# Router transposes in the score tiles' unused columns, the next unit's preparation dealt out anew, and another order for the first head

## The chip, the cores and the metric

The kernel runs on one core of a Trainium2 chip. The metric is the device time of one launch in microseconds; the runs before the change had a median of 1070.12 us (three runs, 1066.64 to 1074.0). TensorE is the matrix engine (PE; PEld its weight loads), VectorE is DVE, ScalarE is ACT, GpSimd is POOL, and SyncE (SP) issues most DMAs.

## The reference

Attention with a threshold feeds a mixture of experts, which feeds a dense layer. The shapes are 4 batches, 8 heads, 576 positions, 64 per head, all float32; 8 experts of 512 x 1024; and a last layer of 512 x 2048 and back.

```python
scores = scale * np.matmul(q, k.transpose(0, 1, 3, 2))
thresh = np.max(scores, axis=-1, keepdims=True) - tau
scores = np.where(scores >= thresh, scores, -1000000000.0)
scores = scores - np.max(scores, axis=-1, keepdims=True)
attn = np.exp(scores)
attn = attn / (np.sum(attn, axis=-1, keepdims=True) + 1e-09)
x = np.matmul(attn, v)                   # then (4*576) rows of 8*64
logits = x @ w_gate
expert_idx = np.argmax(logits, axis=1)   # one expert per row
# out[row] = gate_w[row] * (relu(x[row] @ w1[e]) @ w2[e])
h = x @ w_in
g = h - np.tanh(h)
return (g @ w_out).astype(np.float32)
```

## The kernel before

The program first runs attention (`Attn.run`), then the router's tables, then expert and last layer (`Mlp.run`). The experts need the router's result for all rows, so the second part starts when attention and the logits are done.

**Units and steps.** A unit is one head of two batches at once; there are 16 units. A unit has nine score tiles of 128 x 576, so attention has 144 steps, counted here as (unit, tile). A score tile lies in PSUM as two banks of 512 columns, of which the scores take 288 each; there are three such tiles. In the pass of the main loop with number `i`, these are emitted in this order: jobs of phase 0; `scores` of step i+2 on TensorE; jobs of phase 1; `smax` (maximum, VectorE) and `sexp` (exponential, ScalarE) of step i+1; every third pass `ev_m` (ScalarE copies transposed probabilities out of a score tile's columns 288 to 479); `smask` of step i (VectorE: threshold, multiplication and sum); `sthr`; jobs of phases 2 and 3. Each engine works through its own instructions in the order in which they are emitted, and the framework adds the waits. Two engines that read the same score tile in PSUM are put one behind the other.

**Jobs and their places.** `PL` gives each job of a unit a place (offset, phase), where the offset counts passes from the unit's step 0 (pass 9n for unit n). `PFIRST` replaces places for unit 0, `PLAST` for unit 15. The jobs:

- `lq`, `lk`, `lv`: loads of q, k and v for four heads at once, on SyncE's queue (4, 4 and 6 DMAs); the raw q and k tiles have three buffers.
- `dq` (GpSimd) writes q twice side by side; `hi1` (ScalarE) and `lo1` (GpSimd) split k into a high and a low part.
- `q0`, `m`, `q4`, `k0`, `k5`: transposes on TensorE, four of 128 x 128 (`m` two), into the single PSUM buffer `t`. `e...` is the evacuation on ScalarE, `f...` VectorE's low part of q. The buffer is free again after them.
- `vm`, `vn`, `vc`: maxima of v, their sum and a scale (VectorE, TensorE). `vw`, `vh` (ScalarE) scale v and copy it to fp16, `vl` (GpSimd) makes the low part.
- `se` (ScalarE) and `sl` (GpSimd) split the masked probabilities into two fp16 parts (`e16`, three buffers); `te` transposes them by DMA, three times a unit, also on SyncE's queue. `pv` (TensorE) multiplies by v; `po0` to `po2` (VectorE) put the normalised output into `X`; `st` stores it.
- `t0`, `v0`, `l0` and so on, once per pair of units, after the odd one: the router. `lg_tr` transposes three of nine blocks of `X` into the same buffer `t`, `lg_ev` copies them out (ScalarE, 384 columns), `lg_mm` multiplies by the gate's weights, `la` adds the logits up. They stand at offsets 23 to 32 of the odd unit n, so in units n+2 and n+3.

The places of `PL` that matter below, as step within the unit in which they run: `hi1` 3, `k0` and `ek0` 4, `k5` 4, `ek5` 5, `vw` 4, `vh` 5, `vl` 6, `q0` 7, `eq0` 8, `fq0` 8, `m` 8, `em` 0, `fm` 0, `q4` 0, `eq4` and `fq4` 1, `dq` 3, `lo1` 5.

At the start, `tau` is loaded by GpSimd's queue, unit 0's q by four DMAs of SyncE and its k by four of ScalarE; unit 0's transposes go into score tiles. At pass 4 `consts` makes the router's constants on GpSimd, and VectorE casts them.

## Time and profile before

| | |
|---|---|
| median of three runs | 1070.12 us (1066.64 to 1074.0) |
| the profiled execution | 1065.54 us, span 1063.8 us |
| busy share of the span: PE, DVE, ACT, POOL | 88%, 82%, 68%, 56% |
| mean granted clock of TensorE | 0.958 of full speed |

The profile is of one execution. Busy times are of the union of an engine's instructions. "Idle before" is the time that the engine stood ahead of an instruction, and the name behind the arrow is what ended that wait by the profile; where several things were waited for it is the one that the profile saw last, which need not be the one that mattered. Matmuls overlap, so a row of several matmuls is shorter than the sum of their durations.

### The profile page before, as it was taken

To read this page: it belongs to the slowest core of one execution; us is meant where nothing else is said; L and a number is where in the kernel's file an instruction comes from. 1 tells how busy PE (TensorE), PEld (TensorE's weight loads), DVE (VectorE), ACT (ScalarE), POOL (GpSimd) and SP (SyncE) were. 2 spreads that over 40 slices of the span, in tenths; PEclk is the share of its full clock that TensorE was granted. 3 is DMA by queue.
4 is the path that set the end of the run, shared out by engine and by line. 5 is a ranking of instruction groups with operands and counts; after the bars stand their busy time and mean duration, and the time that the engine had idled before them with its cause. 6 is when DMAs were issued, how large, how long until landed. Compare 5 with 4: busy or idle time off the path is not lost.

```text
span 1063.8 us, 20919 instructions
## 1 busy us (share of the span) xinstructions
PE 940.9 (88%) x7441; PEld 869.2 (82%) x7441; DVE 872.7 (82%) x1667; ACT 721.4 (68%) x1359; POOL 597.0 (56%) x581
## 2 busy tenths in 40 slices
PE   4577787887787498999999998999999999999997
PEld 4466676776786398999999997889999999999986
DVE  5789979888985678786777787999989889898893
ACT  4698998897995175666676766666666566556662
POOL 2788877887876211120011027786867768677763
PEclk9699988998998599999999999999999999999999
DMA  5599999998979497786898875120101001000000
GB/s 138 106 194 170 174 184 180 173 188 182 147 142 170 119 311 251 252 264 223 273 307 279 281 255 171 46 77 21 48 1 42 26 21 48 1 30 1 21 11 31
DMA packets 230826, 147.85 MB, mean 139 GB/s; under 512 B 161306, under 2 KB 207660, under 8 KB 230717
## 3 DMA queue, kind: packets, MB, share of 16 engines
q1 hardware_dynamic: 226957, 135.68, 51.2%
q0 software_dynamic: 3312, 10.49, 3.1%
q8 instruction: 60, 0.98, 0.4%
q14 instruction: 49, 0.40, 0.1%
q10 hardware_dynamic: 448, 0.30, 0.1%
HBM read 85.08 MB, written 23.60 MB: 102 GB/s over the span
## 4 chain that ended last, share of the span: by engine, by line
PE 46%; DVE 10%; DMA 5%; ACT 2%; issue 2%; another core or an unknown queue 0%; SPq 0%; POOL 0%; POOLq 0%; DVEq 0%; ACTq 0%
PE h L1054 22%; PE y L1137 15%; PE y L1109 8%; DMA raw<-in_moe_w_dram 3%; DVE w L1255 2%; DVE w L1256 2%; DMA wscr<-cm 1%; DVE w L1024 1%; DVE w L1253 1%; DVE tm L1254 1%; DVE w L1257 1%; PE t L1031 1%; ACT w L1022 0%; DVE cm L1185 0%; DVE keep L584 0%
## 5 line engine op out<-in xcount | busy, mean ns | idle before, releaser
L267 POOL TENSOR_TENSOR e<-em,e 128x1024 f16<-128x1024 f32 (+1 forms) x98 | 158.1, 1614 | 61.1 <-issue 29.9
L1252 POOL TENSOR_SCALAR tm<-u 128x384 uint8<-128x384 f32 x88 | 128.9, 1465 | 50.2 <-ACT u L1248 49.6
L1054 PE MATMUL h<-xa,w 128*128 128x256 f32 (+6 forms) x864 | 139.3, 311 | 3.3 <-DVE hbuf L1090 1.3
L1109 PE MATMUL y<-hbuf,w 128*128 128x256 f32 (+6 forms) x864 | 139.8, 310 | 0.3 <-ACT yo L1112 0.2
L1054 PEld LDWEIGHTS h<-xa,w 128*128 128x128 f32 x864 | 129.7, 193 | 5.2 <-DVE hbuf L1090 1.8
L255 DVE SCALAR_TENSOR_TENSOR em<-sps,n,e 128x576 f32<-128x576 f32 x144 | 116.8, 811 | 15.8 <-ACT et L287 4.8
L1109 PEld LDWEIGHTS y<-hbuf,w 128*128 128x128 f32 x864 | 127.4, 190 | 1.2 <-ACT yo L1112 0.8
L1248 ACT ACTIVATE u<-h 128x384 f32<-128x384 f32 x96 | 47.1, 491 | 117.5 <-PE h L1054 117.5
L242 ACT ACTIVATE e<-sps,n 128x576 f32<-128x576 f32 x144 | 108.5, 754 | 26.3 <-DVE n L236 26.1
L1255 DVE SCALAR_TENSOR_TENSOR w<-y,w 128x384 f32<-128x384 f32 x96 | 122.5, 1276 | 0.0
L1071 POOL DMA_INDIRECT xr<-rows,idx x26 | 27.3, 1049 | 163.8 <-PE t L1031 158.8
L236 DVE TENSOR_REDUCE n<-sps 128x1 f32<-128x576 f32 x144 | 107.2, 744 | 11.1 <-PE sps L228 11.1
L311 PE MATMUL ops<-vh,et 128*128 128x64 f16 (+1 forms) x2240 | 94.9, 200 | 20.7 <-DVE x L317 20.7
L1054 PE MATMUL h<-xk,w 128*128 128x384 f32 x576 | 109.2, 337 | 2.0 <-DVE w L1024 1.7
L311 PEld LDWEIGHTS <-et 128*128 128x128 f16 (+1 forms) x2240 | 84.1, 106 | 31.1 <-issue 25.7
L1054 PEld LDWEIGHTS h<-xk,w 128*128 128x128 f32 x576 | 102.1, 188 | 6.7 <-DVE w L1024 2.4
L1269 POOL TENSOR_TENSOR gl<-w,gh 128x384 fp32r<-128x384 f32 x83 | 84.6, 1019 | 38.8 <-ACT gh L1268 38.8
L228 PE MATMUL sps<-ka,qa 128*128 128x288 f32 x320 | 84.5, 356 | 19.2 <-DVE n L246 9.1
L263 ACT CAST e<-em 128x576 f16<-128x576 f32 x144 | 98.8, 687 | 3.3 <-DMA et<-e 1.2
L1024 DVE TENSOR_TENSOR w<-raw,w 128x1024 fp32r<-128x1024 f32 x68 | 84.0, 1238 | 20.6 <-ACT w L1022 19.9
L1022 ACT CAST w<-raw 128x1024 fp32r<-128x1024 f32 x72 | 75.4, 1050 | 18.7 <-DVE free L611 11.9
L1256 DVE SCALAR_TENSOR_TENSOR w<-y,w 128x384 f32<-128x384 f32 x96 | 77.7, 809 | 10.0
(237 smaller groups left out, 2207.6 us busy)
## 6 DMA issues: line engine op xcount, KB each, us to landing
raw<-in_moe_w_dram SPq DMA_DIRECT2D x64, 512.0 KB
cv<-in_moe_w_in_dram SPq DMA_DIRECT2D x16, 512.0 KB
cv<-in_moe_w_out_dram SPq DMA_DIRECT2D x16, 512.0 KB
wscr<-cm SPq DMA_DIRECT2D x32, 256.0 KB
raw<-wscr SPq DMA_DIRECT2D x16, 512.0 KB
xw<-yT SPq DMA_DIRECT2D x24, 192.0 KB
vv<-in_v_dram SPq DMA_DIRECT2D x8, 512.0 KB
raw<-in_k_dram SPq DMA_DIRECT2D x6, 512.0 KB
```

What stands on the lines that cost most here:

```text
L236: nc.vector.tensor_reduce(out=n[:, 0:1], in_=ps[:, :, 0:288], axis=AX.XY, op=ALU.max, negate=True)
L242: nc.scalar.activation(out=e, in_=ps[:, :, 0:288], func=AF.Exp, bias=n[:, 0:1])
L255: nc.vector.scalar_tensor_tensor(out=self.em[u, g][:, i].rearrange("p (a b) -> p a b", a=2), in0=ps[:, :, 0:288], scalar=n[:, 1:2], in1=e, ...
L263: self.nc.scalar.copy(self.e16[u, g][:, i, 0:S], self.em[u, g][:, i])
L267: eng.tensor_tensor(out=e16[:, r, S + 64:], in0=em[:, r, 0:512], in1=e16[:, r, 0:512], op=ALU.subtract)
L311: nc.tensor.matmul(o[q], lhsT=et[:, base + c, q], rhs=vh[:, a, j, c if c < 5 else c - 5, :], start=(n == 0), stop=(n == len(terms) - 1))
L1054: self.nc.tensor.matmul(out, lhsT=a, rhs=b, start=(i == 0), stop=(i == len(parts) - 1))
L1109: nc.tensor.matmul(self.ys[d], lhsT=a[:, f % 2, s], rhs=b, start=(f == 0 and i == 0), stop=(f == 7 and i == 2))
L1137: nc.tensor.matmul(self.ys[m], lhsT=a[:, s], rhs=b[:, f % 2], start=(f == 0 and i == 0), stop=(f == 15 and i == 2))
L1252: nc.gpsimd.tensor_scalar(out=mk, in0=u, scalar1=RCUT * RCUT, scalar2=None, op0=ALU.is_gt)
L1255: V.scalar_tensor_tensor(out=w, in0=y, scalar=b, in1=w, op0=ALU.add, op1=ALU.mult)
L1256: V.scalar_tensor_tensor(out=w, in0=z, scalar=d, in1=w, op0=ALU.add, op1=ALU.mult)
```

## The change

The router: for the pairs whose work ends before attention does (odd units 1 to 11), five passes (offsets 22, 23, 25, 26, 28) transpose two, two, two, two and one of the nine blocks of `X` into columns 288 to 415 of the two banks of the score tile that the pass fills, ahead of the scores; these passes are not those of the probability transposes. One pass later ScalarE copies them out, right behind that tile's exponential; another pass later the gate's matmuls run. The pairs of units 13 and 15 keep the old way.

The preparation of the next unit: new places in `PL`; loads of q and v are issued four and six passes earlier. As step within the unit in which they run: `dq` 1, `lo1` 4, `q0` 6, `eq0`, `fq0` 7, `m` and `hi1` 8, `em`, `fm` 0, `q4` 1, `eq4`, `fq4` 2, `vw` 3, `k0` 3, `ek0` and `k5` 4, `ek5` 5, `vh` 6, `vl` 7.

The first head: its q comes in two DMAs instead of four, the loads are emitted ahead of the activation table's load, q's doubling is cut between VectorE and GpSimd, k0 is transposed before `m` and `q4`, and `ek0` goes to ScalarE. The instructions that use tau stand behind the copies of zeros.

```diff
--- before.py
+++ after.py
@@ -27,6 +27,7 @@
...
 MLAG = 3, 4
+LGS = 22, 23, 25, 26, 28
...
@@ -47,22 +48,18 @@
...
+        self.load_qk(0, 0, 0, 1, nc.sync)
+        self.load_qk(0, 1, 0, 1, nc.scalar)
+        t = one.tile([128, 1], F32, name="tau")
+        nc.gpsimd.dma_start(out=t, in_=tau.to_broadcast([128, 1]))
...
         nc.vector.memset(w, 0.0)
         nc.scalar.activation(out=w, in_=w, func=AF.Exp)
-        t = one.tile([128, 1], F32, name="tau")
-        nc.gpsimd.dma_start(out=t, in_=tau.to_broadcast([128, 1]))
-        self.load_qk(0, 0, 0, 1, nc.sync)
-        self.load_qk(0, 1, 0, 1, nc.scalar)
...
-        self.g8 = one.tile([128, 1], F32, name="g8")
-        nc.vector.tensor_scalar(out=self.g8, in0=t, scalar1=0.0, scalar2=0.125, op0=ALU.is_ge, op1=ALU.mult)
-        self.ntau = one.tile([128, 1], F32, name="ntau")
-        nc.vector.tensor_scalar(out=self.ntau, in0=t, scalar1=0.0, scalar2=-1.0, op0=ALU.max, op1=ALU.mult)
...
@@ -71,6 +68,10 @@
                 tl = one.tile([128, 2 * QS], F32R, name=f"{nm}{i}")
                 nc.vector.tensor_copy(tl[:, S:S + 64], z)
                 lst.append(tl)
+        self.g8 = one.tile([128, 1], F32, name="g8")
+        nc.vector.tensor_scalar(out=self.g8, in0=t, scalar1=0.0, scalar2=0.125, op0=ALU.is_ge, op1=ALU.mult)
+        self.ntau = one.tile([128, 1], F32, name="ntau")
+        nc.vector.tensor_scalar(out=self.ntau, in0=t, scalar1=0.0, scalar2=-1.0, op0=ALU.max, op1=ALU.mult)
...
@@ -92,7 +93,7 @@
...
             if i == 0:
                 src = src.rearrange("h (p c) d -> p h c d", c=9)
-                for c in (slice(0, 5), slice(5, 9)):
+                for c in (slice(0, 5), slice(5, 9)) if e1 - e0 > 1 else (slice(0, 9),):
                     eng.dma_start(out=r[p, e0:e1, c], in_=src[:, :, c])
...
@@ -126,7 +127,12 @@
...
     def double(self, u):
         self.xq[u] = self.wk.tile([128, 9, 2, D], F32, tag="xq", name="xq")
-        (self.nc.gpsimd if u else self.nc.vector).tensor_copy(self.xq[u], self.raw[u, 0].unsqueeze(2).to_broadcast([128, 9, 2, D]))
+        src = self.raw[u, 0].unsqueeze(2).to_broadcast([128, 9, 2, D])
+        if u == 0:
+            self.nc.vector.tensor_copy(self.xq[u][:, 0:4], src[:, 0:4])
+            self.nc.gpsimd.tensor_copy(self.xq[u][:, 4:9], src[:, 4:9])
+        else:
+            self.nc.gpsimd.tensor_copy(self.xq[u], src)
...
@@ -198,8 +204,6 @@
...
         if what[0] in "qm":
             nc.scalar.copy(self.qview(self.QA[u % 2], what), self.pview(pf, what))
-        elif u == 0 and what == "k0":
-            nc.vector.tensor_scalar(out=ka[:, 0, 0:512], in0=flat, scalar1=self.g8, scalar2=None, op0=ALU.mult)
...
             nc.scalar.activation(out=ka[:, int(what == "k5"), 0:512], in_=flat, func=AF.Copy, scale=self.g8)
...
@@ -208,11 +212,13 @@
         self.nc.vector.tensor_tensor(out=self.qview(self.QB[u % 2], what), in0=self.pview(pf, what),
                                      in1=self.qview(self.QA[u % 2].bitcast(F32), what), op=ALU.subtract)
...
-    def scores(self, u, t, m=None):
+    def scores(self, u, t, m=None, l=None):
...
         ps = self.sp.tile([128, 2, 512], F32, tag="s", name="sps")
         if m:
...
+        if l:
+            l[0].lg_tr2(ps, *l[1:])
         qa, qb, ka = self.QA[u % 2], self.QB[u % 2], self.ka[u]
         if t == 4:
             terms = [(j, 512 + 64 * j) for j in range(2)]
@@ -331,17 +337,17 @@
...
-    PL = {"lq": (-21, 1), "lk": (-31, 2), "lv": (-12, 1), "dq": (-15, 1), "hi1": (-15, 3),
-          "lo1": (-13, 3), "q0": (-11, 1), "eq0": (-10, 1), "fq0": (-10, 2), "m": (-10, 2), "em": (-9, 1), "fm": (-9, 3), "q4": (-9, 3),
-          "eq4": (-8, 0), "fq4": (-8, 2), "k0": (-5, 0), "ek0": (-5, 0), "k5": (-5, 2), "ek5": (-4, 0),
-          "vm": (-7, 3), "vn": (-3, 1), "vc": (-3, 2), "vw": (4, 3), "vh": (5, 3), "vl": (6, 1),
+    PL = {"lq": (-25, 1), "lk": (-31, 2), "lv": (-18, 1), "dq": (-17, 1), "hi1": (-19, 1),
+          "lo1": (-14, 1), "q0": (-12, 1), "eq0": (-11, 0), "fq0": (-11, 2), "m": (-10, 1), "em": (-9, 0), "fm": (-9, 2), "q4": (-8, 1),
+          "eq4": (-7, 0), "fq4": (-7, 2), "k0": (-6, 1), "ek0": (-5, 0), "k5": (-5, 1), "ek5": (-4, 0),
+          "vm": (-7, 3), "vn": (-3, 1), "vc": (-3, 2), "vw": (3, 0), "vh": (6, 1), "vl": (7, 1),
           "se": (1, 2), "sl": (2, 0), "te": (4, 2), "pv": (11, 3), "po0": (14, 2),
           "po1": (20, 3), "po2": (20, 3), "de": (9, 3), "rc": (13, 1), "st": (32, 3), "t0": (23, 1), "v0": (24, 1), "l0": (31, 2),
           "t1": (24, 3), "v1": (24, 3), "l1": (28, 3), "t2": (29, 0), "v2": (29, 2), "l2": (30, 1), "la": (32, 2)}
...
-    PFIRST = {"dq": (-20, 2), "hi1": (-18, 0), "lo1": (-18, 1), "q0": (-17, 0), "eq0": (-16, 2), "fq0": (-16, 3),
-              "m": (-15, 3), "em": (-14, 1), "fm": (-14, 2), "q4": (-17, 3), "eq4": (-14, 0), "fq4": (-14, 2), "k0": (-15, 3), "ek0": (-13, 2),
-              "k5": (-14, 1), "ek5": (-12, 0),
+    PFIRST = {"dq": (-20, 2), "hi1": (-20, 3), "lo1": (-19, 0), "q0": (-18, 0), "k0": (-17, 1), "m": (-17, 2), "eq0": (-16, 0), "fq0": (-16, 1),
+              "ek0": (-16, 2), "em": (-15, 0), "q4": (-15, 1), "eq4": (-15, 2), "fm": (-15, 2), "k5": (-14, 1), "fq4": (-14, 2),
+              "ek5": (-14, 3),
               "lv": (-2, 1), "vm": (3, 3), "vn": (7, 1), "vc": (7, 2), "vw": (7, 3), "vh": (8, 3), "vl": (8, 3)}
...
@@ -355,7 +361,7 @@
     def run(self, units, moe=None):
...
-        sched = {}
+        sched, lgs = {}, {}
...
@@ -402,7 +408,13 @@
             at(b, "de", self.denom, u)
...
-            if moe and u % 2 == 1:
+            if moe and u % 2 == 1 and b + LGS[-1] + 2 < 9 * NU:
+                P, j = u // H, u % H // 2
+                for x, i in enumerate(LGS):
+                    lgs[b + i] = moe, P, j, x
+                    sched.setdefault((b + i + 2, 3), []).append((moe.lg_mm2, (P, j, x)))
+                at(b, "la", moe.lg_add, P, j)
+            elif moe and u % 2 == 1:
                 P, j = u // H, u % H // 2
...
@@ -419,12 +431,14 @@
...
             if 0 <= i + 2 < len(steps):
                 j = i - MLAG[0]
-                ps[i + 2] = self.scores(*steps[i + 2], (steps[j][0], steps[j][1] // 3) if j >= 0 and j % 3 == 0 else None)
+                ps[i + 2] = self.scores(*steps[i + 2], (steps[j][0], steps[j][1] // 3) if j >= 0 and j % 3 == 0 else None, lgs.get(i))
...
             if 0 <= i + 1 < len(steps):
                 nn[i + 1] = self.smax(ps[i + 1])
                 ee[i + 1] = self.sexp(ps[i + 1], nn[i + 1])
+            if i - 1 in lgs:
+                moe.lg_ev2(ps[i + 1], *lgs[i - 1][1:])
             j = i - MLAG[1]
             if 0 <= j < len(steps) and j % 3 == 0:
                 if i + 2 - MLAG[1] + MLAG[0] >= len(steps):
@@ -485,7 +499,7 @@
     def __init__(self, tc, at, wg, w1, w2, w_in, w_out, out, rows, yT, cp, dp):
...
-        self.cp, self.dp, self.xT, self.wgd = cp, dp, {}, wg
+        self.cp, self.dp, self.xT, self.xT2, self.wgd = cp, dp, {}, {}, wg
...
@@ -565,6 +579,20 @@
...
+
+    def lg_tr2(self, ps, P, j, x):
+        at = self.attn
+        for i in range(min(2, 9 - 2 * x)):
+            self.nc.tensor.transpose(ps[:, i, 288:416], at.X[4 * P + j][:, 2 * x + i], at.ident)
+
+    def lg_ev2(self, ps, P, j, x):
+        n = min(2, 9 - 2 * x)
+        self.xT2[x] = self.attn.wk.tile([128, 3, 128], F32, tag="xT", name="xT", bufs=3)
+        self.nc.scalar.copy(self.xT2[x][:, 0:n], ps[:, 0:n, 288:416])
+
+    def lg_mm2(self, P, j, x):
+        for i in range(min(2, 9 - 2 * x)):
+            self.nc.tensor.matmul(self.attn.lm[:, 2 * x + i], lhsT=self.xT2[x][:, i], rhs=self.wg[:, j], start=True, stop=True)
```

## Rows read from the trace of the kernel before

**Rows 1.** By unit: length, then PE, PEld, DVE, ACT, POOL busy, clock, DMA.
```profile
63.29:82.00 18.71, 13.45 (x213) 12.11 (x210) 16.41 (x44) 16.84 (x31) 15.85 (x17) 1.00 1.11 216
102.79:120.86 18.07, 15.29 (x235) 14.36 (x231) 16.66 (x45) 17.22 (x32) 15.27 (x16) 1.00 0.83 144
120.86:142.44 21.58, 16.45 (x219) 14.88 (x216) 16.38 (x45) 17.79 (x33) 16.47 (x18) 0.84 1.06 218
160.50:183.08 22.58, 16.56 (x221) 14.87 (x218) 20.00 (x51) 17.68 (x33) 16.11 (x18) 0.85 0.92 173
201.15:222.48 21.33, 16.98 (x224) 15.51 (x224) 16.53 (x44) 17.88 (x33) 16.48 (x18) 0.85 1.11 219
240.53:263.36 22.83, 17.06 (x221) 15.39 (x218) 19.75 (x52) 17.70 (x33) 16.26 (x18) 0.85 0.84 175
281.41:301.08 19.67, 15.34 (x220) 13.96 (x216) 16.39 (x45) 17.71 (x33) 16.50 (x18) 0.91 0.83 141
350.21:1063.80 713.59, 677.58 (x3905) 629.19 (x3905) 588.01 (x918) 440.00 (x854) 340.35 (x270) 0.98 0.39 126
```

**Rows 2.** Waits of VectorE in attention: total us, times, longest.
```profile
DVE n L236 <- PE sps L228: 9.6, 14, 1.5
DVE em L255 <- ACT et L287: 4.8, 11, 0.8
DVE pm L132 <- DMA vv<-in_v_dram: 4.8, 3, 2.4
```

**Rows 3.** The timeline of unit 5's middle: start, us, engine.
```profile
131.42 0.67 ACT L263 CAST e<-em 128x576 f16<-128x576 f32 x1 [0.99 <-POOL e L268]
...
133.45 0.90 PE L563 MATMUL lps<-ident,x 128*128 128x128 f32 x3 [2.40 <-ACT ka L204]
...
134.12 0.82 DVE L255 SCALAR_TENSOR_TENSOR em<-sps,n,e 128x576 f32<-128x576 f32 x1 [1.77 <-issue]
```

**Rows 4.** The timeline of unit 8's middle.
```profile
192.40 0.48 ACT L287 COPY et<-sps 128x384 f16<-128x384 f16 x1
...
192.91 0.82 DVE L255 SCALAR_TENSOR_TENSOR em<-sps,n,e 128x576 f32<-128x576 f32 x1 [0.36 <-ACT et L287]
...
193.33 0.85 ACT L146 ACTIVATE vv<-vv,sc 128x640 f32<-128x640 f32 x1
...
194.63 0.76 ACT L242 ACTIVATE e<-sps,n 128x576 f32<-128x576 f32 x1
...
195.48 0.82 DVE L255 SCALAR_TENSOR_TENSOR em<-sps,n,e 128x576 f32<-128x576 f32 x1 [0.55 <-POOL x L124]
...
195.82 0.76 ACT L150 CAST vh<-vv 128x640 f16<-128x640 f32 x1
```

**Rows 5.** Groups by line in attention: busy us, mean ns, idle before.
```profile
L255 DVE SCALAR_TENSOR_TENSOR em<-sps,n,e 128x576 f32<-128x576 f32 x140 | 113.6, 811 | 15.8 <-ACT et L287 4.8 <-POOL x L124 4.4 <-issue 4.1
...
L236 DVE TENSOR_REDUCE n<-sps 128x1 f32<-128x576 f32 x138 | 102.7, 744 | 9.6 <-PE sps L228 9.6
...
L228 PE MATMUL sps<-ka,qa 128*128 128x288 f32 x304 | 79.4, 353 | 16.0 <-DVE n L246 8.8 <-DVE em L255 6.6
...
L228 PE MATMUL sps<-ka,qb 128*128 128x288 f32 x304 | 66.5, 310 | 0.0
...
L563 PE MATMUL lps<-ident,x 128*128 128x128 f32 x63 | 14.6, 355 | 8.6 <-ACT ka L204 7.1 <-ACT xT L567 1.1 <-ACT et L287 0.4
...
L567 ACT COPY xT<-lps 128x384 f32<-128x384 f32 x21 | 10.2, 485 | 2.4 <-PE lps L563 2.3
```

**Rows 6.** The timeline as the constants begin.
```profile
27.93 1.13 POOL L129 COPY xq<-raw 128x1152 f32<-128x1152 f32 x1
...
29.66 0.17 DVE L503 CAST i<-i_i 128x8 f32<-128x8 int32 x1 [2.56 <-POOL i_i L502]
```

**Rows 7.** The timeline of the first loads.
```profile
7.59 2.57 SPq L96 DMA_DIRECT2D raw<-in_q_dram  x4
...
15.43 1.14 POOL L129 COPY xq<-raw 128x1152 f32<-128x1152 f32 x1 [12.83 <-DMA raw<-in_q_dram]
```

## The prediction, made before the change was run

> **What bounds the kernel now.** I read the stretch-by-stretch table first, cut where each attention unit's first mask starts. The part after attention takes 713.59 us and no line of it is edited [rows 1]; everything that can move lies ahead of it, and it starts when attention ends, so a microsecond saved there is one saved in all. In attention no engine is far from full. An even unit takes 18.07 us with ScalarE busy 17.22 and VectorE 16.66 (unit 4; units 6, 8, 10 and 12 repeat it within 0.02). An odd unit should differ little, yet units 5 and 9 take 21.58 and 21.33 with VectorE no busier (16.38 and 16.53), and TensorE's clock is 0.84 and 0.85 there instead of 1.00 [rows 1]. So an odd unit loses about 3.5 us that no engine works in.
>
> Next, who VectorE waits for: score tiles 9.6 us, the small copy of the transposed probabilities on ScalarE 4.8, the load of v 4.8 [rows 2]. The timeline of unit 5 then shows the chain: ScalarE's split waits 0.99 for its buffer, falls behind, and its evacuation of `k5` comes late; the router's transposes (L563) need the one preparation buffer in PSUM, wait 2.40 for that evacuation, and being ahead of the next scores in TensorE's queue they hold these up; VectorE's mask has already stood 1.77 [rows 3]. TensorE then restarts at the low level: three transposes take 0.90.
>
> Even units show the second cause [rows 4]. ScalarE gets v's scaling (0.85) and v's fp16 copy (0.76) in two neighbouring steps, with `ek0` and `ek5` between. Its exponentials come late and the masks wait 0.36 and 0.55. The 0.55 is put down to a GpSimd subtraction, but the exponential that this mask needs runs 194.63 to 195.39 and the mask starts at 195.48: ScalarE is the cause.
>
> **The change part by part.** *Router.* Of the eight odd units, six (1, 3, 5, 7, 9, 11) go the new way; their work falls in units 3 to 14. Nine transposes a pair stay nine, but move from the preparation buffer into columns 288 to 415 of score tiles, two at a time. What goes is the wait for that buffer: 8.6 us of TensorE idle ahead of L563 [rows 5], and with it the low clock. What comes: TensorE does two transposes between a tile's release and its scores. A transpose is 14.6/63 = 0.23 us of busy time, a tile's four score matmuls 2 x 79.4/304 + 2 x 66.5/304 = 0.96 [rows 5]; together 1.42. VectorE's own step (mask and maximum) is the room for it, 0.811 + 0.744 = 1.56 [rows 5], so it fits, barely, at the high clock. ScalarE copies five times (four of 256 columns, one of 128) instead of three times 384 columns at 485 ns [rows 5]. By columns alone nothing is added (9 x 128 either way); at 485 each it is 5 - 3 = 2 more, 0.97 a pair. I take 0.4 a pair, 0.2 a unit, nearer the first end since the tiles are smaller.
>
> A tile with a router copy may also be masked only after that copy: the copy of the transposed probabilities starts at 192.40, behind the exponential on ScalarE, and ends at 192.88; the mask of the same tile starts at 192.91 [rows 4]. The Trainium skill, page "PSUM — Partial Sum Buffer", section Terms, says that two engines may not be on one bank and quadrant at once, "reads against reads included"; the trace's 0.36 agrees. That rule speaks against the change and comes back as a rival.
>
> *Unit preparation.* All its transposes now stand right behind a step's scores, its evacuations at the head of the next step and the low parts behind that step's mask, two steps from one transpose to the next. In `before` `m` and `q4` are queued right behind the low part that frees their buffer. The instructions are the same. On ScalarE v's scaling goes one step earlier and v's copy one later, `hi1` to where only the usual work stands. On GpSimd `dq` and `lo1` move out from in front of the probability splits that the DMA transposes wait for, `vl` goes one step later. I cost the moves at nothing; their cover is VectorE's own 16.7 us a unit. On SyncE the q load (four DMAs) moves four steps up, v's (six) six steps, past one or two DMA transposes each. The DMA transposes that they are moved ahead of come later by the issue (four q issues take 2.57 [rows 7]), and the probabilities they bring are used seven steps later, some 14 us. From q load to its first use there were six steps and are eight; from v load to its first maximum five and eleven. So the 4.8 us for v goes; nothing is late next there.
>
> *Start.* In `before` GpSimd doubles q of unit 2 for 1.13 us right ahead of the constants, and VectorE stands 2.56 us for those [rows 6]. The doubling now is emitted two steps earlier, when GpSimd idles: -1.1. Unit 0's own doubling is cut between two engines, q is loaded in two DMAs instead of four, and its transposes run k first; all that brings the first scores forward. But unit 1's `q0` transposes now stand ahead of the first scores, and they need a load that landed only at 15.43 [rows 7]. Bounds: if that load lands no sooner, the early masks are up to 3 us late and part of it reaches the constants, +1; if it lands a microsecond sooner, -2.5. I take -1.1, the doubling alone, which is in a row. The other edits there (the scalars from tau behind the zero copies, the loads ahead of the table load, `ek0` of unit 0 on ScalarE instead of VectorE) lie inside these ends.
>
> *Sum.* A unit cannot be shorter than its busiest engine. I set each at that plus 0.3 (0.2 for the copies, 0.1 for waits left): even 17.2 + 0.3 = 17.5; odd 17.8 + 0.3 = 18.1; units 7 and 11, where VectorE also takes v's maxima, 20.0 + 0.3 = 20.3 [rows 1]. Savings: units 4, 6, 8, 10, 12 five times 0.57 = 2.8; unit 2 18.71 - 17.5 = 1.2; unit 5 3.5; unit 9 3.2; unit 13 19.67 - 18.1 = 1.6; unit 7 22.58 - 20.3 = 2.3; unit 11 22.83 - 20.3 = 2.5. Units 1, 3, 14 and 15: nothing. That is 17.1, with the start 18.2. The profiled execution took 1065.5 (span 1063.8 and 1.7 around it), so 1047.3; the median of the runs is 4.6 above it, and the same difference from the median gives 1070.1 - 18.2 = **1052**.
>
> **The rivals.** *Copies in score tiles bind* (the PSUM rule above, as a mechanism of this kernel). 30 score tiles carry a router copy. If each holds its mask as the probability copy does, 4.8/11 = 0.44 us [rows 2], that is 13 us, and only 5 of the 18 are left: 1065. For it: ScalarE is 95% busy, so exponentials do not come early. Against: the wait in the timeline stands right where ScalarE is held up by v's work and `ek0`, `ek5` [rows 4], which the change spreads.
>
> *The DMA engines bind.* The shares are 1.06 and 1.11 in units 5 and 9 [rows 1], where k, q or output rows are moved beside the transposes, and the 0.99 wait in unit 5 [rows 3] is for a buffer that a DMA transpose reads last, whatever the row puts it down to. If that, not the router, sets units 5 and 9, their 6.7 us stay: 1059. Against: unit 2 has 1.11 and takes 18.71, unit 13 has 0.83 and loses time all the same.
>
> *TensorE late, and slower than before.* The 1.42 us fits under 1.56 at the high clock only. Where TensorE has stood, matmuls run at the low level (three transposes 0.90 [rows 3] against 3 x 0.23). If the pair ahead of the scores makes VectorE wait at each router tile, the clock falls there as in units 5 and 9, and router tiles now lie in even units too. Six even units at 21.4 instead of 18.06 cost 20; odd units gain nothing; v's 4.8 and the start's 1.1 still go: 1070 + 20 - 6 = 1084. It decides as soon as the path passes 1.56 us, 10% more than I sum. Against: TensorE's other burden, standing behind the preparation buffer, goes.
>
> **How the numbers follow.** Forecast 0.60, at 1045 to 1058 (the start's bounds and 0 to 0.6 in place of 0.3 a unit). Copies 0.12 at 1065; DMA 0.15 at 1059; TensorE 0.08 at 1084; 0.05 for a gain over 25 us. A measurement here tells a change from none at about 1%, 10.7 us, so faster means below 1059.4: 0.60 + 0.05 and two thirds of the DMA case, 0.75. Slower: 0.08. The rest, 0.17, is within 1%. The range 1040 to 1066 leaves out the TensorE case and the far ends.
>
> **What would show it.** Right: even units at 17.3 to 17.8 and odd ones at about 18, ScalarE 96% busy or more; no v wait; no wait of router transposes for an evacuation before unit 15; clock 1.00 through most of attention. Copies: masks that start at the end of a router copy, 30 times. DMA: splits on ScalarE that wait for buffers. TensorE: reductions that wait for scores in the router's steps, at half clock. Wrong start: the constants' first cast on VectorE no earlier than 29.66. The prediction would be wrong above all if ScalarE, with little room, turns each late copy into a late exponential.

## The result and the profile after

The changed kernel took 1053.11 us (median of four runs, 1051.51 to 1054.02) beside 1070.86 us for the kernel before; the ratio (time over the time before) is 0.984, with a 95% interval of 0.981 to 0.987. In a later session it was 0.988 (0.986 to 0.991; 1053.66 beside 1067.08). So the kernel became 1.2 to 1.6% faster, where 1052 was forecast. The profiled execution took 1051.51 us, with a span of 1049.8.

The total fits, its parts do not. The stretch-by-stretch table of the changed kernel, cut as in [rows 1] where each unit's first mask starts; columns as there, for units 2, 4, 5, 6, 10 and 13, and last the stretch from the last mask to the end:

```profile
59.32:80.71 21.39, 16.44 (x223) 15.21 (x221) 16.47 (x44) 16.93 (x31) 17.31 (x18) 0.84 1.15 199
...
101.11:117.73 16.62, 14.38 (x223) 13.63 (x222) 16.44 (x45) 16.62 (x33) 15.65 (x16) 1.00 0.79 137
117.73:136.58 18.85, 15.56 (x226) 14.12 (x224) 16.45 (x45) 17.46 (x34) 16.06 (x17) 1.00 1.10 226
136.58:156.16 19.58, 16.07 (x232) 15.16 (x232) 16.66 (x44) 17.39 (x33) 15.88 (x16) 0.91 1.14 222
...
210.22:230.55 20.33, 16.10 (x232) 15.21 (x232) 16.57 (x44) 17.20 (x33) 15.88 (x16) 0.92 1.12 218
...
267.68:284.79 17.11, 14.66 (x225) 13.88 (x224) 16.35 (x44) 17.03 (x33) 16.05 (x17) 1.00 0.91 161
...
317.66:1049.80 732.14, 692.34 (x4087) 643.22 (x4087) 591.27 (x929) 443.16 (x860) 340.57 (x275) 0.97 0.40 126
```

Unit 4 is at 16.62 (8 and 12 are within 0.07 of it), shorter than the 17.5 forecast, and ScalarE is busy in all of it. Units 5, 7, 9 and 11 (table below) lost 2.3 to 3.7 us, about as forecast. But units 2, 6 and 10, which were to shrink, grew from 18.71, 18.06 and 18.05 [rows 1] to 21.39, 19.58 and 20.33, with the clock down to 0.84 to 0.92.

The waits of the changed kernel in attention (us in all, times, longest) say what ends them:

```profile
DVE qb L212 <- ACT qa L206: 5.7, 4, 2.2
DVE n L242 <- PE sps L234: 4.0, 5, 1.1
...
DVE em L261 <- ACT xT L591: 1.8, 5, 0.4
...
ACT e L269 <- DMA et<-e: 9.5, 7, 2.1
```

The wait for v [rows 2] is gone, and of the 4.8 for the copy of the transposed probabilities 0.2 is left. Two waits have grown: VectorE's for the next unit's q on ScalarE, which was 0.6 us, and ScalarE's split for a DMA transpose, 9.5 us where the kernel before has this row:

```profile
ACT e L263 <- DMA et<-e: 1.0, 2, 0.8
```

The timeline of the changed kernel's unit 6 joins the two. Read it backwards: VectorE stands 1.11 us for `eq4`, which ScalarE could not start because the split ahead of it stood 0.91 us for a DMA transpose. That transpose is the first of the two at 132.23, right behind the q load on SyncE's queue.

```profile
129.44 2.62 SPq L97 DMA_DIRECT2D raw<-in_q_dram  x4
132.23 10.32 SPq L279 DMA_TRANSPOSE et<-e  x2
...
140.88 0.67 ACT L269 CAST e<-em 128x576 f16<-128x576 f32 x1 [0.91 <-DMA et<-e]
...
141.46 0.58 ACT L206 CAST qa<-tps 128x512 fp32r<-128x512 f32 x1
...
142.07 0.69 DVE L212 TENSOR_TENSOR qb<-tps,qa 128x512 fp32r<-128x512 f32 x1 [1.11 <-ACT qa L206]
```

In the chain of work that ended last, four of the five longest pieces are now such transposes (start, us). Each started right behind other transfers on SyncE's queue: the v load at 70.27, k and the row stores at 120.72, the q load at 132.23 and 206.76.

```profile
70.27 8.39 DMA et<-e
120.72 7.32 DMA et<-e
132.23 8.57 DMA et<-e
206.76 8.63 DMA et<-e
```

The start: the constants' first cast on VectorE now waits 0.98 instead of 2.56 [rows 6], and unit 0 takes 23.64 instead of 25.88.

```profile
26.87 0.17 DVE L517 CAST i<-i_i 128x8 f32<-128x8 int32 x1 [0.98 <-POOL i_i L516]
```

### The profile page after: what moved, and what is told of

Same layout as the page of the kernel before. It is cut to its first block, busy times and chain, and to the rows that moved or that the text cites. A ratio compares the mean times of both kernels' runs of the same rounds, so it can differ in the third digit from the quotient of the medians.

```text
span 1049.8 us, 20946 instructions
## 1 busy us (share of the span) xinstructions
PE 935.1 (89%) x7441; PEld 867.8 (83%) x7441; DVE 872.3 (83%) x1666; ACT 720.2 (69%) x1372; POOL 595.9 (57%) x582
## 4 chain that ended last, share of the span: by engine, by line
PE 51%; ACT 17%; DVE 16%; DMA 9%; issue 6%; POOL 1%; ACTq 0%; POOLq 0%; DVEq 0%; SPq 0%
PE h L1082 23%; PE y L1165 15%; PE y L1137 8%; ACT e L248 6%; DMA et<-e 5%; ACT e L269 3%; DVE w L1283 2%; DVE w L1284 2%; DVE n L242 1%; DVE em L261 1%; ACT qa L206 1%; PE ops L317 1%; DVE w L1052 1%; ACT et L293 1%; DVE w L1281 1%
## 5 line engine op out<-in xcount | busy, mean ns | idle before, releaser
L248 ACT ACTIVATE e<-sps,n 128x576 f32<-128x576 f32 x144 | 110.7, 769 | 15.7 <-DVE n L242 15.2
L269 ACT CAST e<-em 128x576 f16<-128x576 f32 x144 | 101.2, 704 | 12.9 <-DMA et<-e 9.5
L1052 DVE TENSOR_TENSOR w<-raw,w 128x1024 fp32r<-128x1024 f32 x68 | 84.3, 1243 | 17.6 <-ACT w L1050 17.4
L234 PE MATMUL sps<-ka,qa 128*128 128x288 f32 x320 | 82.2, 348 | 14.6 <-DVE em L261 7.3
```

The source lines that it names most:

```text
L248: nc.scalar.activation(out=e, in_=ps[:, :, 0:288], func=AF.Exp, bias=n[:, 0:1])
L269: self.nc.scalar.copy(self.e16[u, g][:, i, 0:S], self.em[u, g][:, i])
```

## The experiments

Three questions: which part brings the gain; what makes units 2, 6 and 10 longer; and are the rivals (copies, TensorE) there at all. Ratios are to the kernel before on the same chip. The time before the first mask varies by itself (18.85 to 21.36 us over eight profiles of kernels that do the same up to there), so the profiles are compared by the time from the first mask to the last, "mask to mask", and by units (from one first mask to the next, us):

| profile | mask to mask | units 2, 6, 10 | 4, 8, 12 | 5, 9, 13 | 7, 11 |
|---|---|---|---|---|---|
| before | 314.43 | 18.71 18.06 18.05 | 18.07 18.07 18.06 | 21.57 21.33 19.66 | 22.58 22.82 |
| after | 298.81 | 21.39 19.59 20.34 | 16.63 16.69 16.62 | 18.84 17.59 17.12 | 19.77 20.50 |
| after, once more | 298.07 | 21.06 20.01 20.09 | 16.71 16.70 16.71 | 18.52 18.33 17.12 | 19.78 19.77 |
| v's last steps old in unit 15 | 304.34 | 22.28 19.98 20.63 | 16.54 16.54 16.71 | 19.80 17.92 17.13 | 21.91 20.00 |
| router transposes twice | 301.74 | 22.10 21.50 21.95 | 16.54 16.54 16.54 | 18.57 17.45 17.13 | 20.06 19.96 |
| router alone | 313.18 | 18.42 18.27 18.18 | 17.81 17.81 18.18 | 19.07 19.02 18.39 | 26.48 22.33 |
| places alone | 305.99 | 21.52 19.12 23.38 | 17.42 17.41 17.41 | 19.50 19.00 17.19 | 20.61 19.71 |
| start alone | 316.30 | 18.46 18.06 18.05 | 18.06 18.07 18.06 | 21.07 21.29 21.10 | 23.44 22.59 |
| all but the router | 305.06 | 21.14 19.59 22.98 | 17.39 17.40 17.40 | 19.28 19.02 17.19 | 20.17 19.70 |
| both loads at old places | 297.11 | 18.47 17.32 17.71 | 16.69 16.69 16.69 | 18.50 18.10 17.11 | 23.09 23.36 |
| v load at old place | 299.08 | 20.06 19.73 19.40 | 16.69 16.70 16.70 | 18.40 18.81 17.12 | 21.36 21.52 |
| q load two passes later | 303.02 | 22.90 21.50 21.41 | 16.69 16.63 16.69 | 19.04 17.71 17.12 | 20.44 19.77 |
| q in two DMAs | 300.68 | 22.26 20.59 21.19 | 16.72 16.71 16.70 | 18.61 18.06 17.13 | 19.77 19.78 |
| and stores earlier | 306.10 | 21.09 23.79 25.11 | 16.64 16.64 16.71 | 17.45 17.45 17.13 | 20.50 19.77 |

The second, third and fourth line are of one program up to unit 14 (the fourth changes only unit 15), and their "mask to mask" is 298.1 to 304.3: units 2, 3, 5 and 7 differ by 1.2 to 2.1 us from execution to execution, units 6, 9, 10 and 11 by 0.4 to 0.8, the others hardly. So a few us there say nothing by themselves; 17.4 against 16.6 in units 4, 8 and 12, or 18.5 against 21 in unit 2, do.

### The parts one by one

**The router alone** (the kernel before with `LGS`, `lg_tr2`, `lg_ev2`, `lg_mm2`, nothing else).

> The kernel before with the router's part alone: transposes in score tiles, old places for the preparation, old start. If the router's wait for the preparation buffer makes the odd units long, units 5, 9 and 13 fall from 21.6, 21.3 and 19.7 us to about 18.5 and the time falls by 8 to 10 us; units 7 and 11 keep their wait for v's load and even units their 18.06. Rival, the crowded ScalarE and the late DMA transposes make them long: these units stay above 20.5 and the time falls by less than 4 us.

1065.76 us, ratio 0.998 (0.996 to 1.000). Most of the stall of units 5, 9 and 13 is gone, as the first paragraph of the prediction has it: 21.57, 21.33 and 19.66 become 19.07, 19.02 and 18.39. Little of that arrives (2.4 us in the medians, where 8 to 10 were expected), because unit 7 grows from 22.58 to 26.48. The waits of VectorE in that unit and its row of the stretch table:

```profile
DVE n L239 <- PE sps L231: 2.9, 2, 1.8
DVE pm L133 <- DMA vv<-in_v_dram: 2.9, 1, 2.9
```

```profile
158.90:185.37 26.47, 20.67 (x239) 19.56 (x236) 20.20 (x51) 18.15 (x35) 17.07 (x18) 0.74 0.92 172
```

v's load is late as in the kernel before (2.9 us, there 2.4). TensorE stands meanwhile, 3.14 us ahead of a router pair, and a microsecond after it goes on its granted clock is at the lower level (0.50 between 170.6 and 184.0, 1.00 before). Both of VectorE's waits for scores, 2.9 us in all, begin in that stretch, and in both a router pair stands ahead of the scores. The first of them:

```profile
179.62 0.69 PE L583 MATMUL sps<-ident,x 128*128 128x128 f32 x2
...
181.31 0.76 DVE L239 TENSOR_REDUCE n<-sps 128x1 f32<-128x576 f32 x1 [1.75 <-PE sps L231]
```

That is what the third rival of the prediction describes, a pair of router transposes ahead of the scores at the lower clock, in one unit. In this profile the three units give 6.1 us, and units 3 (22.75 instead of 20.79) and 7 take 5.9 back: some of what the router's stall had cost seems to be only the time by which v came late; that was not tested.

**The new places alone** (the kernel before with the new `PL`). The old router's jobs are moved by a step or two to fit the new preparation, which uses the same buffer: with the old offsets they would stand between a transpose and its own evacuation.

```diff
-    PL = {"lq": (-21, 1), ... "vw": (4, 3), "vh": (5, 3), "vl": (6, 1),
+    PL = {"lq": (-25, 1), ... "vw": (3, 0), "vh": (6, 1), "vl": (7, 1),
-          ... "v0": (24, 1), "t1": (24, 3), "v1": (24, 3), "t2": (29, 0), "v2": (29, 2),
+          ... "v0": (24, 0), "t1": (25, 3), "v1": (26, 0), "t2": (27, 3), "v2": (28, 0),
```

> The kernel before with the new places of the preparation, of v's work and of the loads, and the router in its old form (three transposes at a time through the preparation buffer) at offsets that fit the new places. If the spread of ScalarE's work is what shortens even units, units 4, 8 and 12 fall from 18.06 to 16.6 to 17.0, and v's wait goes (units 7 and 11 about 2.5 us shorter); units 2, 6 and 10 grow by 1.5 to 2.7 as in the changed kernel, because the q load now stands ahead of a DMA transpose; odd units stay long by 2 us or more at the router's places. Sum: 3 to 8 us less than before. Rival, the buffer does not matter once the places are spread: odd units at 17.5 too, and 12 us or more less than before.

1059.98 us, ratio 0.991 (0.988 to 0.993), 8.4 us less from mask to mask. The masks of units 4, 8 and 12 hardly wait (17.41), the wait for v is gone, unit 0 has its 23.64; and units 2, 6 and 10 are already long. So neither the router nor the start is what lengthens them.

One expectation failed here, and it matters: the odd units were to stay long by 2 us or more, since the router still goes through the preparation buffer. Units 5, 9 and 13 took 19.50, 19.00 and 17.19, no more than with the router alone in 9 and 13. Unit 9 of this kernel, and TensorE's wait for the buffer in it:

```profile
196.12:215.12 19.00, 14.19 (x214) 12.68 (x213) 16.63 (x45) 17.42 (x33) 16.06 (x17) 1.00 1.04 210
```

```profile
PE lps L563 <- ACT ka L204: 2.2, 1, 2.2
```

The router's transposes wait 2.2 us for the evacuation of `k`, where they waited 1.6 in unit 9 of the kernel before. Yet VectorE, which stood 3.1 us for scores there, waits for none here, and the clock stays at 1.00. The wait for the buffer alone does not make an odd unit long; it did so together with the old places. Whether the new places of the preparation or those of the router's jobs remove the cost, this run cannot say, as both were moved.

**The start alone** (the kernel before with `PFIRST`, the loads' order, `double` and `ek0`).

> The kernel before with the first head's part alone. In the changed kernel unit 1 starts 3.0 us earlier; of that 1.1 is unit 2's doubling, which is not in this kernel (it belongs to the new places). If the rest is the first head's own, unit 1 starts 1.5 to 2 us earlier here and the time falls by that. Rival, unit 1's preparation swallows it: less than 0.5 us.

1066.73 us, ratio 0.998 (0.997 to 1.000): nothing that can be told from zero. The constants' wait shows why. The first row is of the start alone, the second of the places alone:

```profile
28.91 0.17 DVE L506 CAST i<-i_i 128x8 f32<-128x8 int32 x1 [2.52 <-POOL i_i L505]
```

```profile
28.25 0.17 DVE L503 CAST i<-i_i 128x8 f32<-128x8 int32 x1 [0.98 <-POOL i_i L502]
```

The doubling that stood ahead of the constants is `dq` of unit 2, and it is `PL`, not `PFIRST`, that moves it.

**All but the router** (the changed kernel with every pair on the old router, at the offsets of the second experiment).

```diff
-            if moe and u % 2 == 1 and b + LGS[-1] + 2 < 9 * NU:
+            if False:
```

> The changed kernel with the router in its old form at the same fitted offsets as in the run with the new places alone. If the buffer matters, the odd units grow by 1 to 3 us each and the time is 5 to 10 us above the changed kernel's 1053. Rival: within 2 us of it.

1060.63 us, ratio 0.992 (0.989 to 0.995), the places alone within the uncertainty, so the start adds nothing here either. The new router on top of that is worth what lies between 0.992 and the whole change's 0.984 and 0.988, some 0.4 to 0.8%; the intervals overlap for the second of the two. The 7 us fit what was expected (5 to 10), but they do not lie where they were expected: units 5 and 13 are 0.4 and 0.1 longer than in the changed kernel's first profile and unit 9 1.4, instead of 1 to 3 each. The even units hold most of it: 4, 8 and 12 take 17.40 with the old router and 16.5 to 16.7 with the new, unit 14 takes 16.39 and 15.86, and unit 10, where VectorE waits 3.3 us for scores with the old router and 0.9 with the new, 22.98 and 20.34.

### Units 2, 6 and 10: what is queued ahead of a DMA transpose

**The q load two passes later**, behind the first transpose instead of ahead of it.

```diff
-    PL = {"lq": (-25, 1),
+    PL = {"lq": (-23, 3),
```

> The changed kernel with the q load issued later: two passes and two phases later than in the changed kernel, right behind a DMA transpose instead of ahead of it (the old place is another two passes later). Theory: in units 2, 6 and 10 the q load's four DMAs stand ahead of a DMA transpose on SyncE's queue; the transpose releases the split buffer late, ScalarE's split waits for it (9.5 us in 7 waits), its evacuation of the next unit's q comes late and VectorE waits 1.1 to 2.2 us for that. Then units 2, 6 and 10 fall from 21.4, 19.6 and 20.3 to 17 to 18 us, the split's waits to 2 us or less, and the time by 6 to 10 us, to 1043 to 1047. Rival: the v load, which is issued soon behind, is at fault; then units 6 and 10 stay within 1 us and the time within 2 us of 1053. Second rival: the load is now too late for its own users (doubling on GpSimd): units 1, 5, 9, 13 grow by 1 to 3 us.

1057.76 us, ratio 0.990 (0.987 to 0.993). My theory fell in this form: units 2, 6 and 10 did not shorten (22.90, 21.50 and 21.41), and the splits' waits rose from 9.5 to 16.6 us. The first transpose of unit 5 does start earlier, 12.1 us into the unit (132.56 - 120.47) instead of 14.5 (132.23 - 117.73). The delay only moves down the queue. The timeline of SyncE's queue, and the split at the end of unit 6:

```profile
136.21 3.28 SPq L97 DMA_DIRECT2D raw<-in_q_dram  x4
139.65 5.68 SPq L279 DMA_TRANSPOSE et<-e  x1
...
150.79 9.12 SPq L279 DMA_TRANSPOSE et<-e  x2
...
159.04 0.67 ACT L269 CAST e<-em 128x576 f16<-128x576 f32 x1 [4.49 <-DMA et<-e]
```

From 145.38 to 150.6 the v load is issued, and the transpose that must follow it starts at 150.79, 30.3 us after unit 5 began, where it was 28.9 in the changed kernel.

**The v load at its old place** (`"lv": (-12, 1)`).

> The changed kernel with the v load issued at its old place, six passes later. Theory (the q load alone delays the DMA transposes in units 2, 6 and 10): these units stay within 1 us, and the wait for v comes back in units 7 and 11 (and 3), 1 to 2.5 us each, so the time is 3 to 6 us higher. Rival (the v load delays the transposes): units 2, 6 and 10 fall by 1.5 to 3 us each and the time is the same or up to 4 us lower in spite of the wait for v.

1055.00 us, ratio 0.988 (0.985 to 0.991). Between the two theories: units 2 and 10 are about 1 us shorter, unit 6 no different; the wait for v is back with 3.4 us, and units 7 and 11 are 1.6 and 1.0 longer (unit 7 differs by as much between executions). The time is the same.

**Both loads at their old places**, beside the changed kernel once more.

```diff
-    PL = {"lq": (-25, 1), "lk": (-31, 2), "lv": (-18, 1),
+    PL = {"lq": (-21, 1), "lk": (-31, 2), "lv": (-12, 1),
```

> The changed kernel once more, unchanged, so that the next three and it share a chip. Expected: 1050 to 1055 us, units 2, 6 and 10 at 19.5 to 22.5 us as in all runs with the new places, with splits on ScalarE that wait 9 to 13 us in all for a DMA transpose.

> The changed kernel with both loads, of q and of v, issued at their old places, four and six passes later. Theory A (the loads moved up are what makes units 2, 6 and 10 long): these units fall from about 20.4 to 17.5 to 18.5, the splits' waits for DMA transposes from 9.5 us to under 4, and the wait for v comes back in units 3, 7 and 11, about 2 us each; the time moves by -3 to +2 us. Theory B (SyncE's queue is full over two units whatever the order, since transposes, loads and row stores together need most of it): the length only changes place; the sum of units 5 to 7 stays at 56 to 58 us, and so of 1 to 3 and 9 to 11, and the time within 2 us, or up to 4 us worse.

1053.65 us, ratio 0.988 (0.985 to 0.991), beside 1053.66 and 0.988 for the changed kernel itself, whose splits waited 7.8 us this time. This is the experiment that settles where the loss comes from. Units 2, 6 and 10 fall to 18.47, 17.32 and 17.71, under every profile with the moved loads, so it was the loads' move that made them long. And the wait for v returns in units 7 and 11. The waits of this kernel in attention:

```profile
DVE pm L138 <- DMA vv<-in_v_dram: 6.7, 2, 3.5
...
ACT e L269 <- DMA et<-e: 3.3, 4, 1.7
```

SyncE's queue in units 5 and 6: three transposes go ahead of the q load, and three more ahead of the row stores and the v load, which now are late themselves.

```profile
118.12 12.32 SPq L279 DMA_TRANSPOSE et<-e  x3
130.48 3.30 SPq L97 DMA_DIRECT2D raw<-in_q_dram  x4
133.94 13.93 SPq L279 DMA_TRANSPOSE et<-e  x3
...
150.64 1.28 SPq L110 DMA_DIRECT2D vv<-in_v_dram  x1
```

Theory A holds for where the time is, theory B for what it is worth: units 5 to 7 together take 58.2 us with the new places (18.84 + 19.59 + 19.77) and 58.9 with the old ones, 9 to 11 take 58.4 and 59.2. Only the first three of these heads keep a gain (units 1 to 3: 58.6 and 55.4), which the medians don't show.

**q in two DMAs instead of four**, the same bytes.

```diff
-                for c in (slice(0, 5), slice(5, 9)) if e1 - e0 > 1 else (slice(0, 9),):
+                for c in (slice(0, 9),):
```

> The changed kernel with q of four heads loaded by two DMAs instead of four (same bytes). Theory B (SyncE's queue): 1.3 us of issue less ahead of a DMA transpose, so the split's waits shorten and units 2, 6 and 10 fall by 0.5 to 1.3 us each; the time by 1.5 to 4 us. Rival (the bytes that the DMA engines move beside the transposes are what makes these late): no change, within 1 us.

1054.09 us, ratio 0.988 (0.985 to 0.991): no change, the rival's answer. The first fence is of the changed kernel (its second profile), the second of this one:

```profile
131.04 2.62 SPq L97 DMA_DIRECT2D raw<-in_q_dram  x4
133.81 10.51 SPq L279 DMA_TRANSPOSE et<-e  x2
```

```profile
130.94 1.29 SPq L97 DMA_DIRECT2D raw<-in_q_dram  x2
132.40 12.53 SPq L279 DMA_TRANSPOSE et<-e  x2
```

Issue is 1.33 us shorter, the two transposes behind it 2.02 longer. What the transposes wait out is the load's transfer, 1152 KB either way, and not the time in which it is issued. Whether they stand behind its data in the queue or share the DMA engines with it, these two runs do not tell apart.

**And the row stores seven passes earlier**, on top of the last.

```diff
-          "po1": (20, 3), "po2": (20, 3), "de": (9, 3), "rc": (13, 1), "st": (32, 3),
+          "po1": (20, 3), "po2": (20, 3), "de": (9, 3), "rc": (13, 1), "st": (25, 3),
```

> As the last, and the four stores of a pair's output rows are issued seven passes earlier, in step 7 of an odd unit, so that they no longer fall on the k load's step nor near the v load. Theory B: the queue's 2.5 us of stores leave the stretch that is late (units 4, 6, 8, 10), the transposes there start up to 2.5 us earlier, units 2, 6 and 10 fall by a further 0.5 to 1.5 us, and the time is 3 to 8 us under the changed kernel: 1045 to 1050. Rival: the stores now delay a transpose of the odd unit instead, units 5 and 9 grow, and the time is within 1 us of the last.

1061.68 us, ratio 0.996 (0.994 to 0.997), 7 to 8 us slower than the changed kernel: a miss for both expectations, though the loss lies where the mechanism would put it. The stores do leave the step of the k load, and units 5 and 9 get shorter (17.45). But they now fall right ahead of the v load, and the transpose behind both is the one that the end of unit 6 needs. SyncE's queue and the split:

```profile
141.07 0.61 SPq L335 DMA_DIRECT2D rows<-x  x1
...
143.74 1.29 SPq L110 DMA_DIRECT2D vv<-in_v_dram  x1
...
148.51 24.11 SPq L279 DMA_TRANSPOSE et<-e  x5
...
156.74 0.67 ACT L269 CAST e<-em 128x576 f16<-128x576 f32 x1 [5.66 <-DMA et<-e]
```

Unit 6 goes to 23.79 and unit 10 to 25.11: with two transfers in a row ahead of one transpose they are 3.2 and 3.9 us longer than in the last run.

### The rivals, and the last unit

**Every router transpose twice** (a `for _ in range(2)` around the transpose in `lg_tr2`, the second writing the same values).

> The changed kernel with every router transpose that goes into a score tile done twice (54 transposes more; the second writes the same values). Theory: TensorE has room in these steps, so each doubled pair of 0.46 us is mostly hidden behind VectorE's mask and maximum: the time rises by 0 to 4 us and the mean clock stays at 0.95 to 0.97. Rival (TensorE's path of two transposes and four score matmuls, 1.42 us of 1.56, decides): each of 30 steps is 0.3 us or more longer and the clock falls to half around them, so the time rises by 10 us or more and VectorE's waits for score tiles double.

1054.67 us, ratio 0.987 (0.984 to 0.990); the mean clock is 0.961, against 0.962. Four of a pair's five passes fall in an odd unit, one in the even unit behind it. Unit 13:

```profile
271.20:288.33 17.13, 14.97 (x230) 14.33 (x229) 16.46 (x44) 17.05 (x33) 16.09 (x17) 1.00 1.01 155
```

17.13 us at full clock, where the changed kernel takes 17.11, and units 4, 8 and 12, with one doubled pass each, take 16.54: the added transposes cost nothing there. Units 6 and 10, with one doubled pass too, are 1.3 to 1.9 us longer than in the three profiles of the single transposes; there the clock is low for a time (0.84 in unit 10), and one profile does not tell whether the edit costs it. The median is 1.0 us above the changed kernel's higher one. So TensorE has room at these places at the high clock, and the third rival is out for the changed kernel; its condition, the lower clock, was met in unit 7 of the router alone.

**v's last preparation at its old steps, in the last unit only** (`PLAST` with `vw`, `vh`, `vl` at steps 4, 5 and 6).

> The changed kernel with v's last preparation (scaling, fp16 copy, low part) of unit 15 alone back at its old steps 4, 5 and 6. Theory: at the end of attention GpSimd's subtraction for v's low part and VectorE's subtraction for the last split, both with two SBUF inputs, run side by side; VectorE's takes 2.99 us in the changed kernel against 0.69 before. With the old steps it is 0.7 to 1.0 us again, unit 15 falls from 17.0 to 15.8 to 16.0 and the stretch from the last mask to the end of the span shortens by 1 to 2.4 us; the time is 2 to 3.5 us lower, 1049.5 to 1051. Rival: the end is set by the last DMA transposes or the router's last logits; then the VectorE instruction shortens but the time stays within 0.5 us.

1055.40 us, ratio 0.988 (0.985 to 0.990): no gain. (Up to unit 14 nothing is changed here; the longer units 2, 3 and 7 of its profile belong to the execution.) VectorE's split does shorten, from 2.99 to 0.91 us, but the 64 columns that follow take 1.18 instead of 0.21, and the stretch after the last mask stays (732.12, after 732.14). Unit 15 takes 16.61 instead of 17.00; that need not be the edit, since it takes 16.59 without the edit in the profile with the v load at its old place, where that split took 1.62. What sets the end of attention was not found.

## Why the prediction was right, and where not

**What bounds it: right in part.** Taking the router out of the preparation buffer removes most of the odd units' stall alone (the first experiment). But the new places, with the router still in that buffer and waiting as long for it (7.6 us in all for the evacuation of `k`, 7.1 before), remove as much in units 9 and 13 and nearly as much in unit 5 (the second). So the wait was a link of the chain that the prediction names, ScalarE late, buffer late, scores late; breaking the chain at either link is enough, and the stall is not the router's alone. For the even units the new places alone give 0.65 of the 1.4 us in units 4, 8 and 12, and the router alone 0.26 in units 4 and 8; the rest comes only with both.

**Router: the price right, its place not.** The transposes in score tiles wait for no evacuation and cost nothing measurable on TensorE at the high clock. On top of the new places the new router is worth more in even units, where I had put nothing for it, than in odd ones. ScalarE's five copies take 11.2 us in all over six pairs, 375 ns each, so 1.9 a pair against 1.5 (3 x 485 [rows 5]): the 0.4 that I took. Of the first rival: by the profile only five masks waited for a router copy, 0.23 to 0.43 each, 1.8 us in all, instead of 30 times 0.44. Two more, put down to a GpSimd subtraction (0.38 and 0.22), also start 0.09 us after a copy's end, so it may be 2.4. The price was about right, the number of times was not: ScalarE came early enough. By the rule from the Trainium skill (page "PSUM — Partial Sum Buffer", section Terms) that stands ahead, a copy and a mask may not be on one bank at once; the rows agree, since each of these five masks starts 0.03 to 0.09 us after the copy's end, and none of the 30 starts before it.

**Floor of an even unit: mis-sized.** "A unit cannot be shorter than its busiest engine", and I took ScalarE's busy 17.22 as what a unit cannot go below and added 0.3. Units 4, 8 and 12 came to 16.62 to 16.69, and unit 4 has 33 instructions of ScalarE where it had 32 [rows 1]. Busy time is that of the union, and instructions that follow without a gap overlap. Four of ScalarE's in unit 8 of the changed kernel:

```profile
181.33 0.93 ACT L152 ACTIVATE vv<-vv,sc 128x640 f32<-128x640 f32 x1
182.18 0.74 ACT L248 ACTIVATE e<-sps,n 128x576 f32<-128x576 f32 x1
182.82 0.66 ACT L269 CAST e<-em 128x576 f16<-128x576 f32 x1
183.38 0.69 ACT L208 ACTIVATE ka<-tps,g 128x512 fp32r<-128x512 f32 x1
```

Each starts 0.08 to 0.10 us ahead of the end of the one before it; behind a gap, all of it shows as busy. Over unit 4, the overlaps of ScalarE's instructions sum to 3.25 us in the kernel before and to 4.52 in the changed one. I take this for the difference from 17.22 to 16.62, since no work of ScalarE was removed; it was read, not tested. The term 0.57 a unit measured 1.37 to 1.45 (units 4, 8, 12), and units 1 and 14, which I left at nothing, gave 0.92 and 1.40.

**The loads: the step that failed.** "I cost the moves at nothing; their cover is VectorE's own 16.7 us a unit", and the transposes that come later by the issue had "some 14 us" to spare. The 14 us were counted to the use of the transposed probabilities. The wait is elsewhere: a transpose also frees the `e16` buffer that ScalarE's split needs three groups later, and ScalarE's queue stops there with everything behind it. And the delay is not the issue's 2.57 us [rows 7] but what the load's transfer takes. In place of 1.2, 0.57 and 0.57, units 2, 6 and 10 gave -2.68, -1.53 and -2.29; the saving in units 7 and 11, where the same moves removed the wait for v, was forecast right (2.3 and 2.5, measured 2.81 and 2.32). Undone together, the moves show no difference in time (1053.65 beside 1053.66).

The second rival named the DMA engines, but for units 5 and 9, which did shorten. What it described, splits on ScalarE that wait for buffers, came true in units 2, 6 and 10, and a part of it stayed in unit 5: there the split (at 128.12) still waits 1.31 us for a DMA transpose and VectorE's mask behind it (at 130.36) 1.63.

**Start: the right cause, too small.** Forecast 1.1 for the doubling of unit 2, which `PL` moves. The constants' wait gave 1.58 (2.56 to 0.98), and unit 0 as a whole 2.24, inside the stated bounds; the other 0.66 was not traced. The edits of the first head itself are worth nothing measurable.

**The sum.** From first to last mask 18.2 was forecast and 15.6 measured: too little for units 0, 1 and 14 (by 3.5) and for 4, 8 and 12 (by 2.5), too much for 2, 6 and 10 (by 8.8), the odd ones near (1.5 more in all). Another 1.25 went in unit 15. Ahead of the first mask 0.8 was gained and after the last one 2.4 lost (732.14 after 729.71), and neither is settled: the first differs by 2.5 between profiles of one start, and the second lies between 731.5 and 733.7 in all other profiles, with the old places too (731.5 and 731.7). The medians gained 17.8 and 13.4 us in two sessions, the profile 14.0, all under the forecast's 18.2. So 1052 came out because errors of both signs nearly cancelled; that it came so close was luck.

## What to carry to other kernels

Where one queue carries loads and transposes, a load has two ends: the wait that it relieves if it goes early, and the buffer that comes free late behind it; count to the earliest user of either, and price the load by what its transfer takes, not by its issue. ScalarE's busy time in a stretch with gaps was no floor here: its instructions overlap when they follow without a gap, so add up their spacing where they run dense. Where two changes are made against one stall, run each without the other: here either took most of the odd units' stall away, so neither can be credited with it alone. And where a stall is removed, look at the next thing that is late: the router alone gave 6.1 us in three units, and units 3 and 7 took 5.9 back.

## What the hardware showed that was not expected

**VectorE and GpSimd, each with two inputs in SBUF, hold each other up.** The split of row 6 of the last unit on VectorE, 128 x 512, takes 0.69 us in the kernel before. In the changed kernel GpSimd has three subtractions in a row at that moment, and VectorE's takes 2.99 (rows of these two engines alone):

```profile
314.28 1.40 POOL L160 TENSOR_TENSOR vh<-vv,vh 128x640 f16<-128x640 f32 x1
314.61 2.99 DVE L273 TENSOR_TENSOR e<-em,e 128x512 f16<-128x512 f32 x1 [1.49 <-ACT e L269]
315.64 1.15 POOL L273 TENSOR_TENSOR e<-em,e 128x512 f16<-128x512 f32 x1
316.75 0.30 POOL L274 TENSOR_TENSOR e<-em,e 128x64 f16<-128x64 f32 x1
```

GpSimd's run ends at 317.05, and VectorE's instruction at 317.60, 0.55 later. With v's low part out of the way (the last experiment), its smaller neighbour is caught in the same manner, ending 0.09 us after GpSimd's (the other engine's row first):

```profile
323.42 1.25 POOL L273 TENSOR_TENSOR e<-em,e 128x512 f16<-128x512 f32 x1 [0.31 <-POOL e L274]
```

```profile
323.58 1.18 DVE L274 TENSOR_TENSOR e<-em,e 128x64 f16<-128x64 f32 x1
```

The Trainium skill, page "SBUF — State Buffer", section "Who interferes with whom", says that a VectorE instruction with two SBUF inputs contends with a GpSimd instruction that reads SBUF. These rows agree, and add sizes: 2.3 us more for 128 x 512 here and 1.0 more for 128 x 64. The wait is not always for the whole of GpSimd's run: with the v load at its old place VectorE's 128 x 512 took 1.62 in the same spot, and GpSimd's own next subtraction 1.60 instead of 1.15.

**A transpose behind a load takes the load's transfer with it.** Where nothing is ahead of it, a DMA transpose takes about 3.6 us of SyncE's queue; the one right behind the q load took 6.49 in unit 5 and 6.58 in unit 9 of the changed kernel. In the kernel before it was the same (6.61 in unit 5): the moved loads did not make a transpose behind them slower, they stand ahead of other transposes.
